# One tile for both parts of A, half as many copies, and output stores issued five slots later

## The chip, the cores and the metric

The kernel runs on one core of a Trainium2 chip. The metric is the device time of one execution in microseconds, lower is better. The engines are called by the profile's names: PE (TensorE, the matmuls), DVE (VectorE), ACT (ScalarE), POOL (GpSimd) and SP (SyncE, which here issues nearly all DMAs). SPq is SP's queue of DMA issues.

## The reference

Two attention steps over 32 inducing points, then a feed-forward layer with a leaky ReLU (slope 0.01). `x` is 4 x 12480 x 128, `w_in` 128 x 2048, `w_out` 2048 x 128, the output 49920 x 128.

```python
def mab(q, kv):                       # I is the 32 inducing rows, for each of 4 batches
    s = scale * (q @ kv.transpose(0, 2, 1))
    s = s - s.max(-1, keepdims=True)
    a = np.exp(s)
    a /= a.sum(-1, keepdims=True) + 1e-09
    return a @ kv
h = mab(I, x)                         # 32 x 128 for each batch
y = mab(x, h).reshape(49920, 128)     # attention of each token over 32 rows
t = y @ w_in
out = np.maximum(0.01 * t, t) @ w_out
```

## The kernel before

**What is computed where.** The second attention's weights (32 numbers a token, the matrix A) are not multiplied by h first. The kernel forms h @ w_in for each batch, so that the hidden layer of 512 tokens is a product with the 32 rows of A, and splits each factor into a high and a low part, for three products where one would be too coarse. The leaky ReLU is a ReLU part (`ghi`, `glo`) and a linear part (0.01 t, from A and a product of all weights). On PE a matmul uses a quarter of the array (32 rows), and four streams, r = 0 to 3, take turns on the four quarters; so A must stand in all four groups of 32 partitions.

**Tiles, slots and turns.** A batch has six groups of 2048 tokens (four tiles of 512) and a remainder of 192. The remainders of two batches make a *pair tile*; there are 98 tiles in all, two of them pairs (tiles 28 and 77). The first two tiles ("quick") and the last go another way. For each of the 95 others, the hidden layer is walked in 16 *slots* (f = 0 to 15), about a microsecond each. `row_group(r)` is the order of one stream: "first" makes the hidden part, "second" multiplies it by `w_out`, and first runs four to eight slots ahead of second.

**The background work.** After each slot `next_slot` gives every background lane a step: `stacking`, `stores`, `seconds` (the second attention of later groups), `scores` and `values` (the first attention of the next batch, with its loads `xc` and `xr`). A lane is a list of Python generators; one step runs the first generator to its next `yield`. A lane's step can be put off by `debt` (a heavy step before) and by the quiet slots f = 0 to 3, of which only f = 3 steps `stores`. All this fixes the order of each engine's instructions when the program is built; each engine then runs its own list in order and waits on semaphores.

**The stack.** `stack` takes the four tiles of a group (or one pair): ACT copies the rounded weights into `ahi` (L735), POOL subtracts into `alo` (L740), and for each tile SP copies 32 partitions of each part to the four partition groups of an `A4` tile (L755), eight DMAs a tile. `ahi` and `alo` have one buffer each, so the next stack's L735 and L740 can run only when the copies of the last tile before have landed. There are three `A4` buffers. A pair tile has six parts of 64 tokens, so 48 small DMAs.

**The end of a tile.** `gather` adds the four streams' sums: ACT copies r = 0 and r = 2 into `part` (two buffers), DVE adds r = 1 and r = 3, POOL adds the two. Before a new copy into `part`, it steps the lane of stores until no total is still waiting for its transposition (`while unsaved: step(stores)`). `store` then lets three slots pass, transposes the total on DVE into `osb` (two buffers, L920) and issues four DMAs to the output on SP (L935); 24 small ones for a pair.

Of the kernel before, what the change touches and what calls it, by code (L numbers as in the profile page):

```python
# [9 lines left out]
F32 = mybir.dt.float32  # L10
F32R = mybir.dt.float32r
# [8 lines left out]
def induced_attention_then_leaky_ffn(  # L20
# [20 lines left out]
    nc = tc.nc  # L41
    B, N, C = x.shape
    M = inducing.shape[0]
    DFF = w_in.shape[1]
    P = 128
    NF = DFF // P
    TOK = 512
# [41 lines left out]
    QUICK = 2  # L89
# [3 lines left out]
    GB = 7  # L93
    AHEAD = 4
    LAG = 1
    debt = [0]

    const = ctx.enter_context(tc.tile_pool(name="const", bufs=1))
    sb = ctx.enter_context(tc.tile_pool(name="sb", bufs=2))
# [20 lines left out]
    def done(t, later=6):  # L120
        i = next(i for i in range(8) if banks[i] is t)
        held.discard(i)
        if quads[0]:
            free.append((turn[0] + later, i))
            free.sort()

    def aux_ps(name):
        return bank("aux")
# [593 lines left out]
    def stack(tiles_, eng=None):  # L722

        while not all(s[:2] in aT for t in tiles_ for s in t[1]):
            yield
        ahi = sb.tile([P, TOK], F32R, tag="ahi", name="ahi", bufs=1)
        alo = sb.tile([P, TOK], F32R, tag="alo", name="alo", bufs=1)
        at = {}
        for _, parts in tiles_:
            for b, g, *_ in parts:  # L730
                if (b, g) not in at:
                    at[b, g] = sum(32 * GROUPS[q][2] for _, q in at)
        for (b, g), o in at.items():
            _, J, K = GROUPS[g]
            nc.scalar.copy(ahi[: 32 * J, o : o + 32 * K], aT[b, g][: 32 * J, :])  # L735
        yield
        for (b, g), o in at.items():
            _, J, K = GROUPS[g]
            sl = (slice(0, 32 * J), slice(o, o + 32 * K))
            (eng or nc.gpsimd).tensor_tensor(  # L740
                out=alo[sl], in0=aT.pop((b, g))[: 32 * J, :], in1=ahi[sl].bitcast(F32),
                op=ALU.subtract,
            )
        yield
        for t, parts in tiles_:
            while len(A4) >= A4_BUFS:
                yield
            a4 = sb.tile([P, 2, TOK], F32R, tag="A4", name="A4", bufs=A4_BUFS)
            to = 0
            for b, g, js in parts:  # L750
                w, o = 32 * GROUPS[g][2], at[b, g]
                for j in js:
                    for which in range(2):
                        for r in range(4):
                            nc.sync.dma_start(  # L755
                                a4[32 * r : 32 * r + 32, which, to : to + w].bitcast(F32),
                                (ahi, alo)[which][32 * j : 32 * j + 32, o : o + w].bitcast(F32),
                            )
                    to += w
                    yield  # L760
            A4[t] = a4

    def quick(t):

        b, g, (j,) = tiles[t][0]
        hT = hw[b][0]
        sp = aux_ps("q_ps")
        for c in range(4):
            nc.tensor.matmul(
                sp[:, c * M : (c + 1) * M], xT[b, g][:, j, c * P : (c + 1) * P], hT[:, :M],  # L770
                start=True, stop=True,
            )
        yield
        sv = sp[:, : 4 * M].rearrange("p (c m) -> p c m", m=M)
        mx = sb.tile([P, 4], F32, tag="mx", name="qmx")
        nc.vector.tensor_reduce(out=mx, in_=sv, op=ALU.max, axis=AX.X)
        y = sb.tile([P, 4, M], F32, tag=("ahi", "alo")[t], name="qy", bufs=1)
        nc.vector.tensor_tensor(
            out=y, in0=sv, in1=mx.unsqueeze(2).broadcast_to([P, 4, M]), op=ALU.subtract
        )  # L780
        done(sp)
        nc.scalar.activation(y, y, AF.Exp, scale=SCALE)
        yield
        sm = sb.tile([P, 4], F32, tag="sm", name="qsm")
        nc.vector.tensor_reduce(out=sm, in_=y, op=ALU.add, axis=AX.X)
        nc.vector.tensor_scalar_add(sm, sm, 1e-9)
        nc.vector.reciprocal(sm, sm)
        nc.vector.tensor_tensor(
            out=y, in0=y, in1=sm.unsqueeze(2).broadcast_to([P, 4, M]), op=ALU.mult
        )  # L790
        yield
        pa = bank("out")
        for c in range(4):
            for r in range(4):
                nc.tensor.matmul(
                    pa[32 * r : 32 * r + 32, c * P : (c + 1) * P], y[:, c, :], ident,
                    start=True, stop=True, tile_position=(0, 32 * r),
                )
        yield
        A4[t] = a4 = sb.tile([P, 2, TOK], F32R, tag="A4", name="A4", bufs=A4_BUFS)  # L800
        nc.scalar.copy(a4[:, 0, :], pa)
        yield
        nc.vector.tensor_tensor(
            out=a4[:, 1, :], in0=pa, in1=a4[:, 0, :].bitcast(F32), op=ALU.subtract
        )
        done(pa)
        yield
# [11 lines left out]
    def spans(t):  # L819

        got, at = [], 0
        for b, g, js in tiles[t]:
            n = len(js) * 32 * GROUPS[g][2]
            got.append((b, at, n))
            at += n
        return got, at
# [88 lines left out]
    def store(t, total, summed):  # L915
        _, n = spans(t)
        if summed:
            yield from idle(3)
        osb = sb.tile([P, TOK], F32, tag="osb", name="osb", bufs=2)
        nc.vector.transpose(osb[:, :n], total[:, :n])  # L920
        if summed:
            unsaved.remove(t)
        else:
            done(total)
        yield HEAVY
        o = 0
        for b, g, js in tiles[t]:
            base, J, K = GROUPS[g]
            n = 32 * K
            for j in js:  # L930
                row = b * N + base + j * 32 * K
                dst = out[row : row + n, :].rearrange("(r k) c -> r k c", k=K)
                for cb in range(NB):

                    (nc.scalar if t == NT - 1 and cb % 2 else nc.sync).dma_start(  # L935
                        dst[:, :, 32 * cb : 32 * cb + 32],
                        osb[32 * cb : 32 * cb + 32, o : o + n].rearrange("p (k c) -> p k c", c=32),
                    )
                o += n
            yield  # L940
# [10 lines left out]
    def idle(n):  # L951
        for _ in range(n):
            yield
# [35 lines left out]
    with tc.manual_schedule():  # L989
# [102 lines left out]
        def row_group(r):  # L1092

            todo = []
            for i, (t, f) in enumerate(work):
                if f % 4 == r:
                    todo.append((i - AHEAD - FURTHER * (r == FAR), 0, "first", t, f))
                todo.append((i + LAG * r, 1, "second", t, f))
                if r != t % 4 and f == (3 if t > QUICK + 3 else NF - 1):
                    todo.append((i + LAG * r + 0.5, 2, "linear", t, (r - t) % 4 - 1))  # L1100
            todo.sort()
# [70 lines left out]
        t = NT - 1  # L1172
# [45 lines left out]
```

## Time and profile before

| what | value |
|---|---|
| median of three runs | 1670.46 us (1669.81 to 1673.67) |
| the profiled execution's own time | 1674.81 us |
| its span, first to last instruction | 1672.7 us |
| mean granted clock of PE | 0.966 |
| PE busy | 1562.8 us, 93% of the span |
| DVE, ACT, POOL busy | 1163.7, 1066.9, 941.7 us |
| share of the chain that ended last on PE, on the SP queue | 79%, 11% |

A row of groups has the line, engine and operation, the tiles (out<-in), the form and the count, then busy time and mean ns of one, then the idle time before them and what ended it. A row of waits has the total, the number and the longest wait in us. A row of a timeline has start and length in us; x4 means four instructions merged into it, and square brackets hold idle time ahead. A row of windows has, after the window and its length, the busy time and count of PE, PEld (weight loads), DVE, ACT and POOL, then the granted clock, the DMA engines' share and GB/s.

### The profile page before, as it was taken

Reading aid. Unit: us, or ns where it says so; the run is one execution under the profiler, and the core shown is the slowest. Engines: PE = TensorE matmul, PEld = TensorE weight load, DVE = VectorE, ACT = ScalarE, POOL = GpSimd, SP = SyncE. Lnnn points to the kernel's source line nnn. Section 1 sums busy time; section 2 is a strip of 40 time slices with the busy share of each in tenths; the row PEclk is TensorE's granted clock in tenths of the full one; section 3 lists DMA queues with packets and bytes.
Section 4 is the critical chain, followed back from the end, with each engine's and each line's share of the span. In section 5 each row is a group of like instructions: output and inputs, shape, how many; then the busy total and the mean of one; then the engine's idle time right before and its main releaser. Section 6 shows DMA issues by size and latency. Waiting matters only on the chain.

```text
span 1672.7 us, 60122 instructions
## 1 busy us (share of the span) xinstructions
PE 1562.8 (93%) x25047; PEld 1353.4 (81%) x25047; DVE 1163.7 (70%) x2046; ACT 1066.9 (64%) x1957; POOL 941.7 (56%) x963
## 2 busy tenths in 40 slices
PE   8999999999966899999996999999999598999997
PEld 5678888888855778888886888878889497999996
DVE  6677788767744667776774788767777376766664
ACT  6456677676733566666674676667677365777773
POOL 2146666566633555565664675555666465666663
PEclk9899999999977999999998999999999799999998
DMA  7155544422333244443224444553222122222221
GB/s 256 18 116 94 109 100 99 103 54 54 60 79 67 49 96 101 98 90 77 53 51 99 74 81 101 105 120 77 53 51 54 33 45 55 59 59 59 58 47 20
DMA packets 419520, 128.52 MB, mean 77 GB/s; under 512 B 379920, under 2 KB 382384, under 8 KB 419248
## 3 DMA queue, kind: packets, MB, share of 16 engines
q1 hardware_dynamic: 418144, 124.53, 35.8%
q8 instruction: 197, 3.23, 0.8%
q14 instruction: 75, 0.61, 0.1%
q10 hardware_dynamic: 1104, 0.15, 0.1%
HBM read 48.94 MB, written 25.56 MB: 45 GB/s over the span
## 4 chain that ended last, share of the span: by engine, by line
PE 79%; SPq 11%; DMA 3%; DVE 3%; issue 2%; POOL 1%; ACT 1%; ACTq 0%; DVEq 0%; POOLq 0%
PE bank L874 72%; SPq L755 4%; SPq L320 3%; SPq L935 3%; PE bank L334 2%; PE bank L900 2%; PE bank L458 1%; DMA xr<-in_x_dram 1%; DVE glo L852 1%; DMA A<-ahi 1%; POOL glo L845 1%; DMA raw<-in_moe_w_in_dram 1%; ACT ghi L849 0%; DMA A<-alo 0%; PE bank L365 0%
## 5 line engine op out<-in xcount | busy, mean ns | idle before, releaser
L874 PE MATMUL bank<-ghi,w_hi 32*128 32x512 f32 x6080 | 1295.8, 394 | 0.6 <-DVE part L1157 0.4
L874 PE MATMUL bank<-glo,w_hi 32*128 32x512 f32 x6080 | 1295.1, 393 | 0.2 <-DVE glo L852 0.2
L874 PE MATMUL bank<-ghi,w_lo 32*128 32x512 f32 x6080 | 1294.5, 394 | 0.0
L874 PE MATMUL bank<-A,hwhi 32*128 32x512 f32 (+1 forms) x3394 | 1136.0, 394 | 68.1 <-ACT g L842 62.4
L852 DVE SCALAR_TENSOR_TENSOR glo<-bank,ghi 128x512 fp32r<-128x512 f32 x1184 | 796.1, 681 | 350.7 <-ACT ghi L849 344.4
L849 ACT ACTIVATE ghi<-bank 128x512 fp32r<-128x512 f32 x1184 | 701.6, 598 | 296.1 <-PE bank L874 269.8
L874 PEld LDWEIGHTS bank<-ghi,w_hi 32*128 32x128 f32 x6080 | 847.3, 185 | 46.5 <-issue 17.6
L874 PEld LDWEIGHTS bank<-glo,w_hi 32*128 32x128 f32 x6080 | 850.0, 185 | 27.3 <-DVE glo L852 0.6
L874 PEld LDWEIGHTS bank<-ghi,w_lo 32*128 32x128 f32 x6080 | 849.4, 185 | 25.0
L874 PEld LDWEIGHTS bank<-A,hwhi 32*128 32x128 f32 x3394 | 586.2, 185 | 115.1 <-ACT g L842 66.6
L874 PE MATMUL bank<-A,hwlo 32*128 32x512 f32 (+1 forms) x1697 | 642.5, 391 | 0.0
L845 POOL TENSOR_TENSOR glo<-g,ghi 128x512 fp32r<-128x512 f32 (+1 forms) x384 | 495.7, 1291 | 30.7
L844 POOL CAST ghi<-g 128x512 fp32r<-128x512 f32 (+1 forms) x384 | 234.1, 610 | 407.1 <-ACT g L842 339.2
L874 PEld LDWEIGHTS bank<-A,hwlo 32*128 32x128 f32 x1697 | 307.4, 185 | 7.6
L842 ACT ACTIVATE g<-bank 128x512 f32<-128x512 f32 (+1 forms) x384 | 229.4, 597 | 126.3 <-PE bank L874 120.0
L1161 POOL TENSOR_TENSOR part<-part 128x512 f32<-128x512 f32 (+1 forms) x95 | 122.6, 1290 | 109.1 <-DVE part L1157 109.1
L1157 DVE TENSOR_TENSOR part<-bank,part 128x512 f32<-128x512 f32 (+1 forms) x190 | 130.2, 685 | 57.4 <-PE bank L874 46.2
L1154 ACT COPY part<-bank 128x512 f32<-128x512 f32 (+1 forms) x190 | 110.4, 581 | 35.7 <-PE bank L874 35.0
L740 POOL TENSOR_TENSOR alo<-aT,ahi 128x512 fp32r<-128x512 f32 x24 | 31.0, 1291 | 83.0 <-DMA A<-alo 45.8
L735 ACT CAST ahi<-aT 128x512 fp32r<-128x512 f32 x24 | 14.8, 615 | 88.7 <-DMA A<-ahi 78.2
L920 DVE STREAM_TRANSPOSE osb<-part 128x512 f32<-128x512 f32 (+1 forms) x95 | 66.3, 698 | 0.0
L439 DVE STREAM_TRANSPOSE xT<-xc 128x512 f32<-128x512 f32 x72 | 50.3, 698 | 0.0
(120 smaller groups left out, 644.6 us busy)
## 6 DMA issues: line engine op xcount, KB each, us to landing
xr<-in_x_dram SPq DMA_DIRECT2D x96, 256.0 KB, 4.8
out_dram<-osb SPq DMA_DIRECT2D x382, 64.0 KB, 2.2
A<-ahi SPq DMA_DIRECT2D x376, 64.0 KB, 2.0
A<-alo SPq DMA_DIRECT2D x376, 64.0 KB, 2.0
xc<-in_x_dram SPq DMA_DIRECT2D x288, 64.0 KB, 2.7
raw<-in_moe_w_in_dram SPq DMA_DIRECT2D x4, 512.0 KB, 6.7
raw<-in_moe_w_out_dram SPq DMA_DIRECT2D x4, 512.0 KB, 7.4
A<-ahi SPq DMA_DIRECT2D x48, 8.0 KB, 1.8
```

Of the source, the lines that this page charges most:

```text
L439: nc.vector.transpose(t[:, j, :], blk.rearrange("p n c -> p (n c)"))
L755: nc.sync.dma_start(a4[32 * r : 32 * r + 32, which, to : to + w].bitcast(F32), (ahi, alo)[which][32 * j : 32 * j + 32, o : o + w].bitcast( ...
L842: nc.scalar.activation(g[:, :n], ph[:, :n], AF.Relu)
L844: nc.gpsimd.tensor_copy(ghi[:, :n], g[:, :n])
L845: nc.gpsimd.tensor_tensor(out=glo[:, :n], in0=g[:, :n], in1=ghi[:, :n].bitcast(F32), op=ALU.subtract)
L849: nc.scalar.activation(ghi[:, :n], ph[:, :n], AF.Relu)
L852: nc.vector.scalar_tensor_tensor(out=glo[:, :n], in0=ph[:, :n], scalar=0.0, in1=ghi[:, :n].bitcast(F32), op0=ALU.max, op1=ALU.subtract,)
L874: nc.tensor.matmul(dst, w[32 * r : 32 * r + 32], x[32 * r : 32 * r + 32], start=start, stop=stop, tile_position=(32 * r, 0),)
L920: nc.vector.transpose(osb[:, :n], total[:, :n])
L1154: nc.scalar.copy(part[:, :n], po[:, :n])
L1157: nc.vector.tensor_tensor(out=part[:, :n], in0=po[:, :n], in1=part[:, :n], op=ALU.add)
L1161: nc.gpsimd.tensor_tensor(out=total[:, :n], in0=total[:, :n], in1=part[:, :n], op=ALU.add)
```

## The change

`ahi` and `alo` become the two halves of one tile `both`, and one DMA copies both parts of 32 partitions into an `A4` tile: four DMAs of 128 KB a tile where there were eight of 64 KB, and 24 for a pair where there were 48. Quick's two scratch tiles, which used the places of `ahi` and `alo`, share a tile of the new kind. In `store`, five more steps of the lane pass between the transposition and the DMAs.

```diff
+    STORE = 5
...
-        ahi = sb.tile([P, TOK], F32R, tag="ahi", name="ahi", bufs=1)
-        alo = sb.tile([P, TOK], F32R, tag="alo", name="alo", bufs=1)
+        both = sb.tile([P, 2, TOK], F32R, tag="both", name="both", bufs=1)
+        ahi, alo = both[:, 0, :], both[:, 1, :]
...
-                    for which in range(2):
-                        for r in range(4):
-                            nc.sync.dma_start(
-                                a4[32 * r : 32 * r + 32, which, to : to + w].bitcast(F32),
-                                (ahi, alo)[which][32 * j : 32 * j + 32, o : o + w].bitcast(F32),
-                            )
+                    for r in range(4):
+                        nc.sync.dma_start(
+                            a4[32 * r : 32 * r + 32, :, to : to + w].bitcast(F32),
+                            both[32 * j : 32 * j + 32, :, o : o + w].bitcast(F32),
+                        )
...
-        y = sb.tile([P, 4, M], F32, tag=("ahi", "alo")[t], name="qy", bufs=1)
+        if not qys:
+            qys.append(sb.tile([P, QUICK, 4, M], F32, tag="both", name="qy", bufs=1))
+        y = qys[0][:, t]
...
         yield HEAVY
+        if summed:
+            yield from idle(STORE)
         o = 0
```

In the changed kernel the copies stay at L755, the stores stand at L941, the transposition at L924, and gather's copy and add at L1160 and L1163. How the change moves instructions is shown at three places.

SP's queue where the loads of the third batch come in (`xc`, `xr`), ahead of the first pair's copies; before:

```order
L935 DMA out_dram<-osb 512x1x32 x4
L320 DMA xc<-in_x_dram 32x2x32 x12
L320 DMA xc<-in_x_dram 32x16x32 x16
L310 DMA xr<-in_x_dram 96x256
L310 DMA xr<-in_x_dram 128x512 x4
L755 DMA A_9373<-ahi 32x512 x4
L755 DMA A_9373<-alo 32x512 x4
L935 DMA out_dram<-osb 512x1x32 x4
L320 DMA xc<-in_x_dram 32x16x32 x8
L755 DMA A_9731<-ahi 32x512 x4
L755 DMA A_9731<-alo 32x512 x4
```

The same place after:

```order
L941 DMA out_dram<-osb 512x1x32 x4
L321 DMA xc<-in_x_dram 32x2x32 x12
L321 DMA xc<-in_x_dram 32x16x32 x16
L311 DMA xr<-in_x_dram 96x256
L311 DMA xr<-in_x_dram 128x512 x4
L755 DMA A_9282<-both 32x1024 x4
L941 DMA out_dram<-osb 512x1x32 x4
L321 DMA xc<-in_x_dram 32x16x32 x8
L755 DMA A_9638<-both 32x1024 x4
L941 DMA out_dram<-osb 512x1x32 x4
L755 DMA A_10002<-both 32x2x64 x24
```

The rows keep their places, with four copies for eight, but each store is that of the tile before: the first row stores tile 22 before and tile 21 after.

SP's queue at the output of the first pair tile, the 24 small stores; before:

```order
L755 DMA A_11274<-ahi 32x512 x4
L755 DMA A_11274<-alo 32x512 x4
L935 DMA out_dram<-osb 64x1x32 x24
L320 DMA xc<-in_x_dram 32x16x32 x8
L755 DMA A_11663<-ahi 32x512 x4
L755 DMA A_11663<-alo 32x512 x4
```

The same place after:

```order
L755 DMA A_11155<-both 32x1024 x4
L321 DMA xc<-in_x_dram 32x16x32 x8
L941 DMA out_dram<-osb 512x1x32 x4
L321 DMA xc<-in_x_dram 32x16x32 x8
L755 DMA A_11520<-both 32x1024 x4
L311 DMA xr<-in_x_dram 128x512 x4
L941 DMA out_dram<-osb 64x1x32 x24
L755 DMA A_11920<-both 32x1024 x4
```

The 24 stores stood ahead of the copies of tile 32 (A_11663), the last of its stack, and stand behind them now (A_11520).

DVE's list at the gathering of a tile (the adds into `part`, two of each tile) and the transposition of a total into `osb`; before:

```order
L1157 TENSOR_TENSOR part<-bank_67,part 128x512
L852 SCALAR_TENSOR_TENSOR glo<-bank_66,ghi 128x512
L852 SCALAR_TENSOR_TENSOR glo<-bank_69,ghi 128x512
L1157 TENSOR_TENSOR part<-bank_68,part 128x512
L852 SCALAR_TENSOR_TENSOR glo<-bank_71,ghi 128x512
L852 SCALAR_TENSOR_TENSOR glo<-bank_69,ghi 128x512
L852 SCALAR_TENSOR_TENSOR glo<-bank_68,ghi 128x512
L920 STREAM_TRANSPOSE osb<-part 128x512
```

The same place after:

```order
L856 SCALAR_TENSOR_TENSOR glo<-bank_70,ghi 128x512
L856 SCALAR_TENSOR_TENSOR glo<-bank_71,ghi 128x512
L924 STREAM_TRANSPOSE osb<-part 128x512
L1163 TENSOR_TENSOR part<-bank_66,part 128x512
L856 SCALAR_TENSOR_TENSOR glo<-bank_67,ghi 128x512
L856 SCALAR_TENSOR_TENSOR glo<-bank_71,ghi 128x512
L1163 TENSOR_TENSOR part<-bank_64,part 128x512
```

The transposition stood three rows behind a tile's own second add and stands now just ahead of the next tile's first add; in ACT's list one of the next tile's two copies into `part`, the second, now waits for DVE.

More of the change, by code (lines that the diff above doesn't have):

```diff
@@ L761, in stack @@
             A4[t] = a4
+    qys = []
     def quick(t):
```

## The prediction

> **What bounds the kernel now.** First the page's busy shares and the idle time before the groups of TensorE, then the list of waits, then windows cut around the idle places, and last the timeline of the SP queue ahead of them.
>
> ```profile
> PE 1562.8 (93%) x25047; PEld 1353.4 (81%) x25047; DVE 1163.7 (70%) x2046; ACT 1066.9 (64%) x1957; POOL 941.7 (56%) x963
> ...
> ACT ahi L735 <- DMA A<-ahi: 93.9, 8, 18.9
> ...
> PE bank L874 <- ACT g L842: 62.4, 6, 16.7
> ...
> PE bank L334 <- DVE glo L852: 17.8, 1, 17.8
> ```
>
> TensorE is busy for 93% of the span, and what it waits for longest (62.4 us in only six waits, 17.8 in one) are relu results of ACT and DVE. ACT is not slow: it stands at L735, the copy of a new stack's high part, until the DMAs that still read the old stack have landed (93.9 us in eight waits). Nine windows take in every idle place of TensorE after the start that is over 1 us, except the program's end; the last row is a stretch without any.
>
> ```profile
> 461.00:484.00 23.00, 8.70 (x114) 6.91 (x110) 4.68 (x9) 4.65 (x10) 4.25 (x6) 0.64 0.55 117
> 500.00:526.00 26.00, 9.32 (x105) 7.39 (x101) 5.69 (x11) 6.18 (x12) 5.97 (x6) 0.61 0.20 39
> 576.00:594.00 18.00, 7.79 (x96) 6.08 (x88) 4.71 (x9) 4.51 (x9) 4.20 (x5) 0.72 0.46 81
> 654.00:662.00 8.00, 6.49 (x78) 4.72 (x76) 3.15 (x5) 4.26 (x8) 4.95 (x5) 0.79 0.47 95
> 717.00:727.00 10.00, 8.07 (x138) 5.60 (x135) 4.21 (x11) 4.46 (x9) 4.57 (x5) 1.00 0.62 142
> 902.00:925.00 23.00, 9.11 (x123) 8.07 (x120) 5.60 (x10) 5.03 (x11) 5.00 (x5) 0.70 0.57 119
> 1106.00:1116.00 10.00, 6.49 (x92) 3.73 (x88) 3.15 (x9) 2.68 (x5) 3.10 (x3) 0.83 0.52 100
> 1313.00:1338.00 25.00, 7.17 (x88) 4.30 (x84) 2.66 (x5) 3.71 (x8) 5.02 (x5) 0.66 0.19 36
> 1386.00:1400.00 14.00, 7.92 (x108) 6.71 (x104) 3.77 (x7) 3.99 (x8) 4.65 (x6) 0.76 0.35 69
> sum 157.00, PE 71.06 PEld 53.52 DVE 37.63 ACT 39.47 POOL 41.71; mean PE 7.90 PEld 5.95 DVE 4.18 ACT 4.39 POOL 4.63
> ...
> 1475.00:1635.00 160.00, 160.00 (x2750) 153.74 (x2745) 112.75 (x171) 115.82 (x207) 103.45 (x105) 1.00 0.27 55
> ```
>
> The nine windows are 157.0 us long and TensorE is busy for 71.1 of them, so 85.9 us are idle. They hold 942 matmuls (the sum of the counts); at the 2750 in 160 us of the last row, 17.2 a us, these need 54.8 us. So the windows lose 102.2 us: 85.9 idle and 16.3 at the lower granted clock (0.61 to 0.83 in eight of them, 1.00 in the last row). If all of it went, the span of 1672.7 would be 1570.5. The profiled execution took 1674.81 us, 4.35 over the median of 1670.46; I take what is saved off the median, which makes the floor 1568.3.
>
> What the DMAs wait for is the SP queue. Its timeline ahead of the first loss, and ACT's rows at L735 at the six large ones (start, length, then the idle time ahead):
>
> ```profile
> 433.90 3.25 SPq L935 DMA_DIRECT2D out_dram<-osb  x4
> 437.20 20.41 SPq L320 DMA_DIRECT2D xc<-in_x_dram  x28
> 457.65 3.36 SPq L310 DMA_DIRECT2D xr<-in_x_dram  x5
> 461.11 2.44 SPq L755 DMA_DIRECT2D A<-ahi  x4
> 463.60 2.50 SPq L755 DMA_DIRECT2D A<-alo  x4
> 466.19 2.63 SPq L935 DMA_DIRECT2D out_dram<-osb  x4
> 468.87 5.32 SPq L320 DMA_DIRECT2D xc<-in_x_dram  x8
> 474.29 2.47 SPq L755 DMA_DIRECT2D A<-ahi  x4
> ...
> 478.38 0.39 ACT L735 CAST ahi<-aTr 96x64 fp32r<-96x64 f32 x2 [15.74 <-DMA A<-ahi]
> ...
> 517.44 0.62 ACT L735 CAST ahi<-aT 128x512 fp32r<-128x512 f32 x1 [18.48 <-DMA A<-ahi]
> ...
> 587.87 0.62 ACT L735 CAST ahi<-aT 128x512 fp32r<-128x512 f32 x1 [12.58 <-DMA A<-ahi]
> ...
> 919.15 0.62 ACT L735 CAST ahi<-aT 128x512 fp32r<-128x512 f32 x1 [16.25 <-DMA A<-ahi]
> ...
> 1332.28 0.62 ACT L735 CAST ahi<-aT 128x512 fp32r<-128x512 f32 x1 [18.90 <-DMA A<-ahi]
> ...
> 1394.20 0.62 ACT L735 CAST ahi<-aT 128x512 fp32r<-128x512 f32 x1 [8.21 <-DMA A<-ahi]
> ```
>
> SP issues back to back from 433.9 to 476.8, each DMA 0.6 to 0.65 us after the last (2.44 for four, 20.41 for 28). ACT was ready at 478.38 - 15.74 = 462.6, but the last tile of the old stack had its copies issued only from 474.29. TensorE loses about 1.8 us less than ACT waits (15.74 gave an idle 23.00 - 8.70 = 14.3; 18.90 gave 25.00 - 7.17 = 17.8): so much work lies ahead of it.
>
> **The merged copy.** It removes 424 issues on SP, half of all copies: 376 of the whole tiles (row below) and 48 of the two pair tiles. Whether a DMA of 128 KB is issued as fast as one of 64 KB no row shows; the bounds are these:
>
> ```profile
> A<-ahi SPq DMA_DIRECT2D x376, 64.0 KB, 2.0
> ...
> xr<-in_x_dram SPq DMA_DIRECT2D x96, 256.0 KB, 4.8
> ...
> 489.20:510.80 21.60, 13.24 (x227) 10.67 (x223) 9.31 (x16) 7.71 (x15) 7.99 (x8) 0.86 0.07 14
> ...
> 1583.50:1588.50 5.00, 5.00 (x93) 5.00 (x89) 2.90 (x5) 3.86 (x7) 2.36 (x3) 1.00 0.49 109
> ```
>
> Four xr loads of 256 KB and a smaller one took 3.36 us above, 0.67 each with a pause among them: bytes do not set the issue time. I take 0.63 us, so 2.5 us a tile instead of 5.0; the other end is 1.25 us, with nothing saved. Landing lies between 2.0 us (64 KB) and 4.8 (256 KB); I take 2.4, near the first, since the eight copies of a tile, one each 0.63 us, fill only 0.49 of the DMA engines (last row), so twice the bytes in that time just fit. Bytes stay the same in all.
>
> The row of 489.2 to 510.8 is a pair tile's 48 copies of 8 KB: issues at full cadence, and the DMA engines 0.07 busy. The Trainium skill, "DMA: Bandwidth & Descriptors", section "Issuing engines are not separate DMA queues", says that the sequencer's time to start a DMA is usually small beside the DMA itself. By that, halving the issues would bring nothing and only the moved stores count; the 0.07 speaks against it here. The second rival below has the time that this would give.
>
> **The later store.** `store` now takes 11 steps of its lane where it took 6, and a tile has 16 slots, some of them barred. So the next tile's store starts late, `gather` forces its transposition, and the DMAs come a whole tile later than before, against every other queue entry. The SP queue no longer stands waiting for a fresh transposition: ahead of the 28 loads it must now wait for the one that stands at the gathering before (its second ACT copy, the first one at 426.40), not for that at 433.2.
>
> ```profile
> 426.40 0.59 ACT L1154 COPY part<-bank 128x512 f32<-128x512 f32 x1 [0.35 <-PE bank L874]
> 428.71 0.58 ACT L1154 COPY part<-bank 128x512 f32<-128x512 f32 x1
> ...
> 866.49 0.58 ACT L1154 COPY part<-bank 128x512 f32<-128x512 f32 x1
> ...
> L920 DVE STREAM_TRANSPOSE osb<-part 128x512 f32<-128x512 f32 (+1 forms) x95 | 66.3, 698 | 0.0
> ```
>
> The cost is that the second copy into `part` waits for this transposition (it writes the buffer that is read). DVE needs 0.70 us for it and starts it ahead of the first copy's time, so it ends near 427.4, 1.3 us before the second copy at 428.71. Per tile I put the loss at 0.05 us, between 0 and the 0.7 of a transposition that starts when the copy is due; about 75 of the 95 tiles have it so close in the order of the instructions, hence 4 us, with 0 and 52 as ends. `osb` has two buffers and its DMAs now end about 20 slots before the next use instead of 30, so no wait. Quick's shared tile costs nothing: both are read and gone long before the first stack. The final tile's store is not delayed.
>
> **Each loss again, with these prices.** At 462.6: store after the transposition at 427.5, until 430.1; the 33 loads take 461.11 - 437.20 = 23.9, until 454.0; one tile's copies 2.5, a store 2.6, eight loads 5.3, the last tile's copies 2.5, until 466.9, landed near 468.9. ACT waits 6.3, TensorE 4.5. At 902.9 (919.15 - 16.25) the same from 867.5: 2.6, 22.4 (loads and their pauses), 2.5, 2.6, 5.3, 2.5 end at 905.4, landed at 907.4; ACT waits 4.5, TensorE 2.7.
>
> The pair tile: 48 copies become 24. The next rows are the first and the last four high-part copies of the second pair and the 24 stores of its output.
>
> ```profile
> 1298.75 2.46 SPq L755 DMA_DIRECT2D A<-ahi  x4
> ...
> 1328.31 2.49 SPq L755 DMA_DIRECT2D A<-ahi  x4
> ...
> 1373.37 16.54 SPq L935 DMA_DIRECT2D out_dram<-osb  x24
> ```
>
> They can start when the low part is made, near 1296.5; 24 x 0.63 = 15.1 and one store of 2.6 end at 1314.2, landed 1.5 later (now the last are issued by 1330.8 and release ACT at 1332.28): ACT, ready at 1332.28 - 18.90 = 1313.4, waits 2.3, TensorE 0.5 instead of 17.8. The first pair starts once ACT is free at 468.9 and ACT and POOL have split the new stack, 2 us that I estimate from ACT's 0.39; 15.1 on and 1.5 to land make 487.5. ACT gets there at 517.44 - 18.48 = 499.0 now, and 9.8 earlier (14.3 idle become 4.5), at 489.2, then: 0 instead of 16.7. The 24 stores of a pair's output now stand behind the last tile's copies: the loss at 1394 (6.1) goes, that at 588 (10.2) shrinks: 16.5 us of stores leave the queue ahead of ACT's 12.6 us wait, eight loads of 5.3 come in, the copies take 2.5 less, which would end it; as these loads wait for buffers that DVE frees, I leave 0.9. The three small losses (1.5, 1.9, 3.5 idle) lose half of a tile's 5.0 us: 0, 0 and 0.6. Left idle: 4.5 + 2.7 + 0.5 + 0.9 + 0.6 = 9.2. For the clock I leave 1.7 us at three of them, 5.1, as the window of 654 to 662 has it: (1 - 0.79) x 8.
>
> The Trainium skill, "TensorE: Matmul & The Clock Gate", Part 1, has the clock halve only after an idle window of about 3.4 us. By it only the loss of 4.5 would cost clock and the sum would be some 3 us less; the window of 654 to 662, with 1.5 us idle and 0.79, does not agree.
>
> Sum: 102.2 - 9.2 - 5.1 - 4 = 83.9 saved; 1670.5 - 83.9 = 1587.
>
> **Rivals.** First, the transposition at the gathering reaches TensorE at 0.2 to 0.5 us a tile, through DVE running late: 75 tiles make 15 to 37 us, 1601 to 1623. For it: DVE and ACT are near 70% in the clean stretch (112.75 and 115.82 of 160). Against: 1.3 us of room. Second, a merged issue takes twice as long, so only the moved stores help: the boundary waits are each 5 us longer, the pair tiles keep 30 us of issues and idle about 9 and 14, in all some 43 us idle, 9 of clock and 9 for the rest: 41 saved, 1629. Against it are the xr rows. Third, everything goes: 1568 to 1573, if TensorE's lead covers the waits of 4 to 6 us. The one on the other side: DVE reaches the forced transposition so late that TensorE pays each time. That outweighs 88 us from 1.2 us a tile on 75 tiles; at 1.5 it would be 1670.5 - 88 + 112 = 1695. It needs DVE 2.5 us behind at each gathering, which no row here shows. Last, that the store moves without effect and the copies were not on the path: the chain through L735 speaks against it.
>
> **Chances.** Forecast 0.66 (1574 to 1600), first rival 0.12, second 0.10, third 0.07, slower 0.03, within 0.3% (1665.5 to 1675.5, what a measurement tells from none) 0.02. From 1569 to 1628 lie the forecast, the first rival and half of the second and third, over 8 in 10. Faster 0.95.
>
> **What would show it.** Right: SP's merged copies 2.5 us for four; L735's waits under 7 us, two of them left; the window list above with under 12 us idle; the second L1160 copy never waiting over 1 us for DVE. Wrong: four merged copies taking 5 us; waits at L735 that stay over 10; TensorE idle spread over all tiles, released by ACT or DVE.

## The result, and the profile after

| kernel | median, us | range | ratio to before, 95% interval |
|---|---|---|---|
| before | 1672.07 | 1669.81 to 1673.79 | |
| changed | 1620.67 | 1618.41 to 1625.50 | 0.9697 [0.9671, 0.9724] |

The change makes the kernel 3.0% faster, 51 us, where 84 were forecast. The profiled execution took 1625.50 us, with a span of 1623.7 us against 1672.7: 49.0 us less. From the page of the changed kernel, the busy line and the shares of the chain that ended last:

```profile
PE 1571.7 (97%) x25047; PEld 1339.5 (82%) x25047; DVE 1157.0 (71%) x2046; ACT 1068.4 (66%) x1957; POOL 943.3 (58%) x963
...
PE 82%; DVE 6%; POOL 4%; issue 3%; ACT 2%; SPq 1%; DMA 1%; ACTq 0%; DVEq 0%; POOLq 0%
```

The SP queue's share of the chain fell from 11% to 1%; DVE's rose from 3% to 6%. PE is busy for 9 us longer than before, with the same number of matmuls. The waits (total in us, number, longest) show what left and what came:

```profile
PEld bank L878 <- DVE glo L856: 49.7, 75, 3.9
...
ACT both L736 <- DMA A<-both: 23.7, 5, 8.2
...
PE bank L878 <- DVE glo L856: 17.2, 23, 3.4
PE bank L878 <- ACT g L846: 12.9, 5, 5.4
```

ACT's wait for the old stack's copies is down from 93.9 us to 23.7, and PE's wait for ACT's `g` from 62.4 to 12.9. The wait for DVE's `glo` went the other way. Before, these two rows read:

```profile
PEld bank L874 <- DVE glo L852: 23.1, 40, 2.3
...
PE bank L874 <- DVE glo L852: 5.0, 7, 1.9
```

Of the nine windows of the prediction three are left:

```profile
480.00:492.00 12.00, 6.75 (x74) 3.83 (x66) 2.50 (x5) 2.94 (x7) 3.64 (x6) 0.78 0.56 101
884.00:900.00 16.00, 10.61 (x102) 6.67 (x101) 4.22 (x8) 4.37 (x8) 5.59 (x6) 0.68 0.55 105
1289.00:1299.00 10.00, 6.58 (x84) 5.03 (x80) 4.31 (x8) 4.02 (x8) 5.88 (x6) 0.83 0.27 58
```

ACT's timeline has its copies of a new stack in them (start, length, and in brackets the wait):

```profile
487.40 0.39 ACT L736 CAST both<-aTr 96x64 fp32r<-96x64 f32 x2 [8.17 <-DMA A<-both]
...
890.53 0.62 ACT L736 CAST both<-aT 128x512 fp32r<-128x512 f32 x1 [8.18 <-DMA A<-both]
...
1293.27 0.62 ACT L736 CAST both<-aT 128x512 fp32r<-128x512 f32 x1 [4.54 <-DMA A<-both]
```

Counted as in the prediction (17.2 matmuls a us), these 38.0 us hold work for 15.1: lost are 14.1 idle and 8.8 at the lower clock, 22.9 together.

The rest is found tile by tile. The matmuls bank<-ghi,w_hi are 64 to a tile, so that their order gives the time at which each slot began in either kernel. The difference in length between two slots, changed less before, in us:

```
start to slot 48                          +3.2
slots 48 to 400    (22 tiles)            +13.0
slots 400 to 512   (losses at 462 to 588)  -37.4
slots 512 to 800   (losses at 654, 717)    -0.4
slots 800 to 832   (loss at 902)           -5.8
slots 832 to 992                          +2.6
slots 992 to 1008  (loss at 1106)          -4.3
slots 1008 to 1200                        +4.5
slots 1200 to 1280 (losses at 1313, 1386) -24.7
slots 1280 to 1540 (no background work)   +0.3
```

The boundaries gained 72 us, and stretches that had lost nothing before became longer. The clearest is the first, slots 48 to 400 (windows of before, then of the changed kernel):

```profile
114.30:455.10 340.80, 340.09 (x5689) 296.45 (x5685) 262.96 (x460) 236.33 (x432) 214.20 (x219) 1.00 0.41 84
```

```profile
117.50:471.30 353.80, 348.05 (x5695) 289.49 (x5694) 263.44 (x465) 237.52 (x433) 216.01 (x221) 1.00 0.42 83
```

It has the same number of matmuls within 6 and DVE's busy time within 0.5 us, and is 13.0 us longer. Only 5.0 of these are PE's idle time (5.75 against 0.71). Of the other 8 some 1.7 are clock: the 1.00 of the long row is rounded, and from 229 to 236 us the clock was 0.76 (a row at the end of this text shows it). The rest is "busy". Four streams share PE, and while one waits for its `glo` the others go on: PE counts as busy with less of it at work. What DVE did there at a gathering, in the changed kernel (idle time ahead would stand in brackets):

```profile
198.52 0.70 DVE L440 STREAM_TRANSPOSE xT<-xc 128x512 f32<-128x512 f32 x1
199.14 0.67 DVE L924 STREAM_TRANSPOSE osb<-part 128x512 f32<-128x512 f32 x1
199.74 0.65 DVE L1163 TENSOR_TENSOR part<-bank,part 128x512 f32<-128x512 f32 x1
200.31 1.27 DVE L856 SCALAR_TENSOR_TENSOR glo<-bank,ghi 128x512 fp32r<-128x512 f32 x2
201.51 0.67 DVE L1163 TENSOR_TENSOR part<-bank,part 128x512 f32<-128x512 f32 x1
202.11 0.67 DVE L856 SCALAR_TENSOR_TENSOR glo<-bank,ghi 128x512 fp32r<-128x512 f32 x1
202.70 0.69 DVE L440 STREAM_TRANSPOSE xT<-xc 128x512 f32<-128x512 f32 x1
203.38 0.69 DVE L856 SCALAR_TENSOR_TENSOR glo<-bank,ghi 128x512 fp32r<-128x512 f32 x1
```

At a gathering near there before the change, the transposition (L920) stood 5 us behind the second add:

```profile
194.78 0.69 DVE L1157 TENSOR_TENSOR part<-bank,part 128x512 f32<-128x512 f32 x1 [0.45 <-PE bank L874]
195.39 1.34 DVE L852 SCALAR_TENSOR_TENSOR glo<-bank,ghi 128x512 fp32r<-128x512 f32 x2
196.65 0.68 DVE L1157 TENSOR_TENSOR part<-bank,part 128x512 f32<-128x512 f32 x1
...
201.57 0.69 DVE L920 STREAM_TRANSPOSE osb<-part 128x512 f32<-128x512 f32 x1
```

In the changed kernel the forced transposition (L924) and the two adds (L1163) stand within 3.1 us, with background work (L440) on either side, and DVE has no pause in them: five operations of 0.7 us that are not `glo` among four that are. That is theory 1: this clump makes `glo` late. Its rivals were that the background work, which moved to earlier slots too, does it (theory 2; of DVE's 574 background instructions 335 stand in another tile than before), and that the merged copies do (theory 3).

### The profile page after: what moved, and what is told of

Same layout as the page of the kernel before. It is cut to its first block, busy times and chain, and to the rows that moved or that the text cites. A ratio compares the mean times of both kernels' runs of the same rounds, so it can differ in the third digit from the quotient of the medians.

```text
span 1623.7 us, 59550 instructions
## 1 busy us (share of the span) xinstructions
PE 1571.7 (97%) x25047; PEld 1339.5 (82%) x25047; DVE 1157.0 (71%) x2046; ACT 1068.4 (66%) x1957; POOL 943.3 (58%) x963
## 4 chain that ended last, share of the span: by engine, by line
PE 82%; DVE 6%; POOL 4%; issue 3%; ACT 2%; SPq 1%; DMA 1%; ACTq 0%; DVEq 0%; POOLq 0%
PE bank L878 75%; PE bank L335 3%; DVE glo L856 2%; POOL glo L849 2%; PE bank L904 2%; PE bank L459 1%; POOL ghi L848 1%; DVE part L1163 1%; SPq L755 1%; ACT ghi L853 1%; DMA A<-both 1%; POOL y L710 1%; PE bank L366 0%; POOL y L696 0%; DVE e L347 0%
## 5 line engine op out<-in xcount | busy, mean ns | idle before, releaser
L878 PE MATMUL bank<-ghi,w_hi 32*128 32x512 f32 (+1 forms) x6080 | 1294.8, 393 | 2.2 <-DVE glo L856 1.7
L878 PE MATMUL bank<-ghi,w_lo 32*128 32x512 f32 (+1 forms) x6080 | 1292.0, 393 | 0.0
L878 PEld LDWEIGHTS bank<-ghi,w_hi 32*128 32x128 f32 x6080 | 842.1, 184 | 51.1 <-issue 14.3
L1163 DVE TENSOR_TENSOR part<-bank,part 128x512 f32<-128x512 f32 (+1 forms) x190 | 129.2, 680 | 33.5 <-PE bank L878 21.0
L1160 ACT COPY part<-bank 128x512 f32<-128x512 f32 (+1 forms) x190 | 110.5, 581 | 26.1 <-PE bank L878 24.8
L924 DVE STREAM_TRANSPOSE osb<-part 128x512 f32<-128x512 f32 (+1 forms) x95 | 65.9, 694 | 0.0
L440 DVE STREAM_TRANSPOSE xT<-xc 128x512 f32<-128x512 f32 x72 | 50.2, 697 | 0.0
L741 POOL TENSOR_TENSOR both<-aT,both 128x512 fp32r<-128x512 f32 x24 | 31.1, 1295 | 29.2 <-ACT both L736 25.1
L690 DVE STREAM_TRANSPOSE y<-bank 128x512 f32<-128x512 f32 (+1 forms) x28 | 18.1, 647 | 21.3 <-PE bank L335 21.3
```

Of the source, the lines that this page charges most:

```text
L440: nc.vector.transpose(t[:, j, :], blk.rearrange("p n c -> p (n c)"))
L878: nc.tensor.matmul(dst, w[32 * r : 32 * r + 32], x[32 * r : 32 * r + 32], start=start, stop=stop, tile_position=(32 * r, 0),)
L1160: nc.scalar.copy(part[:, :n], po[:, :n])
L1163: nc.vector.tensor_tensor(out=part[:, :n], in0=po[:, :n], in1=part[:, :n], op=ALU.add)
```

## The experiments

**The parts of the change, each alone.** The first kernel has the changed kernel's copies and no delay of the stores; the second has the delay and the eight copies.

```diff
 first kernel: the changed one with
-    STORE = 5
+    STORE = 0
 second kernel: the one before with
+    STORE = 5
...
         yield HEAVY
+        if summed:
+            yield from idle(STORE)
```

> The merged copies alone: the stores follow their transposition at once, as in the kernel before, and every instruction but the A copies stands in the slot where it stood before. Theory 1 (in the changed kernel the transposition is forced onto the gathering of the next tile, DVE's work stands there in a clump and its glo comes late by fractions of a microsecond on many tiles): no clump here, so the clump's 15 to 25 us are not paid, but SP still waits at fresh transpositions and five of the nine windows keep a part of their stall (11.6, 10, 10.7, 6 and 0.5 us, and 11 us of half clock). Worked out: 52 us saved, 1620 us, between 1612 and 1632. The rows would show ACT's wait for the DMAs of the old stack at 35 to 50 us in all (93.9 before) and PE's wait for glo as before (about 5 us on PE, 23 us on PEld). Theory 2 (what is lost is lost to background work that stands earlier in the changed kernel, since the debt of the transposition falls into quiet slots): the same here, since the background stands as before. Theory 3 (the merged copies themselves cost PE, by their bytes or their landing): slower than 1640 us, and PE's small waits as in the changed kernel.

Measured: 1644.36 us (1642.60 to 1646.38), ratio 0.9821 [0.9803, 0.9840]. The waits of ACT and PE:

```profile
ACT both L736 <- DMA A<-both: 70.8, 11, 14.1
...
PEld bank L878 <- DVE glo L856: 23.5, 41, 2.3
...
PE bank L878 <- DVE glo L856: 5.0, 7, 1.8
```

The waits for `glo` are those of before to within 0.4 us, and the stretch of slots 48 to 400 is 0.2 us longer than before, so the merged copies cost PE nothing (theory 3 falls). The size was missed by 24 us: ACT's waits stayed at 70.8 us, where 35 to 50 were expected.

> The later stores alone: eight copies a tile from two tiles, and five slots between the transposition and its stores. Theory 1: the clump is here in full, as in the changed kernel (PE's and PEld's waits for glo about 17 and 50 us, 5 and 23 before), while the copies take 5 us a tile as before; some 41 us of the nine windows go, 15 to 25 us come back: 1650 us, between 1640 and 1662. Theory 2: the same, since the background moves as in the changed kernel. Theory 3 (the merged copies cost PE): no clump, PE's waits for glo as before, 1630 us or less.

Measured: 1659.49 us (1655.13 to 1661.34), ratio 0.9908 [0.9882, 0.9934], inside the range of theories 1 and 2.

```profile
PEld bank L875 <- DVE glo L853: 58.9, 69, 15.6
PE bank L875 <- DVE glo L853: 28.6, 22, 15.1
```

The waits for `glo` rise without a merged copy (one of 15 us among them belongs to a boundary). So the later store pays and costs: 15 us gained alone; the merged copies bring 30 us alone, and some 35 behind later stores (from the ratios 0.9908 and 0.9697; the kernel before was measured anew with each group of runs, and its medians differ by 2.7 us).

**The transposition or the background work.** In the third kernel the stores' DMAs are issued from a lane of their own, so nothing forces the transposition. The fourth is the changed kernel with the debt charged later.

```diff
 third kernel
+        while len(outs) > 1:
+            step(outs)
         osb = sb.tile([P, TOK], F32, tag="osb", name="osb", bufs=2)
...
-            yield from idle(STORE)
+            outs.append(issue(t, osb, STORE + 2 * (len(tiles[t]) > 1)))
+        else:
+            yield from issue(t, osb, 0)
 (issue(t, osb, later) idles `later` steps, then issues the DMAs; STORE = 6;
  the lane outs is stepped once a slot, behind that of the stacks)
 fourth kernel
+        yield
+        if summed:
+            yield from idle(3)
         yield HEAVY
         if summed:
-            yield from idle(STORE)
+            yield from idle(1)
```

> Merged copies and later stores, but the transposition where it stood before: three steps after the sums, not forced by the gathering of the next tile, since the stores have a lane of their own and are issued 8 to 25 slots behind their transposition (13 in the mean, in the changed kernel 10). The background work (loads of xc and xr, scores, values) stands in the slots where it stood before. Theory 1: the relief at the boundaries of the changed kernel is kept and the clump on DVE is gone, so PE's and PEld's waits for glo fall back to about 5 and 23 us; 15 to 25 us faster than the changed kernel, 1600 us, between 1594 and 1608. Theory 2 (it is the background that moved): as fast, since the background stands as before too; the fourth kernel tells the two apart. Theory 3 (neither; the residue belongs to the merged copies or the late stores themselves): within 5 us of the changed kernel, 1616 to 1626 us.

Measured: 1609.17 us (1607.58 to 1609.95), ratio 0.9610 [0.9593, 0.9626]; by the ratios some 14.6 us faster than the changed kernel (11.5 by the medians). The clean stretch of slots 48 to 400 is as long as before the change, 340.70 us:

```profile
116.00:456.70 340.70, 339.99 (x5689) 297.09 (x5685) 263.15 (x460) 236.72 (x432) 214.35 (x219) 1.00 0.45 88
```

Each tile in it is as long as before to 0.1 us. The gain is smaller than the spread price that went, since a new loss came: the first pair's late stores hold an `osb` that DVE needs. PE's and PEld's waits for `glo` are 15.9 and 35.2 us, where about 5 and 23 were expected; 8.3 and 8.7 of them are this one stall.

```profile
575.70 0.71 DVE L926 STREAM_TRANSPOSE osb<-part 128x512 f32<-128x512 f32 x1 [9.22 <-DMA out_dram<-osb]
```

> The changed kernel with one edit: the debt of the transposition is charged three steps of the lane later. The transposition is still forced onto the gathering (77 of 95 within one slot of it, 63 in the changed kernel), the stores stand as late as there, but the background work (xc, xr, scores, values) stands again where it stood in the kernel before (it was 9 to 15 slots earlier in the changed kernel). Theory 1 (the forced transposition): as slow as the changed kernel, 1614 to 1628 us, PE's waits for glo at 17 and 50 us. Theory 2 (the background that moved): 15 to 25 us faster, about 1600 us, between 1594 and 1608, and PE's waits for glo back at 5 and 23 us.

Measured: 1623.08 us (1621.58 to 1625.53), ratio 0.9695 [0.9677, 0.9714], as slow as the changed kernel. In its profile 539 of DVE's 574 background instructions stand in the tile where they stood before, and slots 48 to 400 still take 11.0 us longer. Theory 2 falls as the whole cause: with the background back in its place the price stays while the transposition is forced, and in the third kernel it goes. How much of it hangs on the background's place is not settled: the waits for `glo` fell part of the way (10.1 us on PE and 34.9 on PEld, where 17 and 50 were expected), and ACT has two long waits at a new stack's copy in this stretch (3.06 us at 162.71 and 2.50 at 230.01, where the longest before was 0.70). That the route is DVE's list is read from the rows.

**What the boundaries still cost.** In undisturbed stretches of before, ACT's copy of a new stack starts 5 to 7 us behind the issue of the old stack's last copies, and SP's first copy of the new stack is issued 10 to 15 us behind it. So the copy should be able to stand later with little or nothing needing it:

```diff
 def stack(tiles_, eng=None):
         while not all(s[:2] in aT for t in tiles_ for s in t[1]):
             yield
+        if tiles_[0][0] > 4 + QUICK:
+            yield from idle(4 if len(tiles[tiles_[0][0] - 1]) > 1 else 8)
```

It was put into the kernel before, the merged copies alone (the expectations call this one the eighth kernel), the third kernel and the changed one.

> The kernel before (eight copies a tile, stores behind their transposition) with one edit: the copy of a new stack on ACT, and POOL's subtraction with it, are put eight steps of their lane later (four after a pair), about 8 us. Every other instruction stands in the slot where it stood. The new stack's first copy by SP comes 14 slots after the old stack's last, so nothing needs the copy sooner. Theory A (the whole loss at the boundaries is ACT standing in its list at a copy that nobody needs yet, while SP works off its queue): SP's issues are as slow and as late as before, yet most of the loss goes: of ACT's eight waits, 93.9 us in all, each loses some 8 us, 30 to 40 us stay; saves 65 to 80 us, 1600 us, between 1588 and 1615. Theory B (SP's queue itself bounds these windows, whoever waits for it: if ACT doesn't wait at the old copies, PE waits soon after for the new ones): the loss moves to PE's waits for DMAs into A, and at most 25 us are saved, over 1645 us.

Measured: 1639.85 us (1637.69 to 1642.18), ratio 0.9787 [0.9772, 0.9801]: 35 us faster, between both theories and nearer theory B's bound.

```profile
482.54 0.39 ACT L737 CAST ahi<-aTr 96x64 fp32r<-96x64 f32 x2 [8.09 <-DMA A<-ahi]
...
519.54 0.62 ACT L737 CAST ahi<-aT 128x512 fp32r<-128x512 f32 x1 [21.79 <-DMA A<-ahi]
```

The wait ahead of the pair fell from 15.7 to 8.1 us as theory A has it, but that behind it rose from 18.5 to 21.8: there four steps are too few while SP works off the pair's 48 copies. Theory B's shift is there but small: PE waits for copies into A, for which it hadn't waited before, for 1.7 us in all.

> Merged copies alone (stores behind their transposition at once, the transposition where it stood before) and ACT's copy of a new stack eight steps of the lane later. Theory A: ACT's waits for the old stack's copies, 70.8 us in 11 with the merged copies alone and at most 14.1, fall to under 10 us; no clump on DVE and no late store; 1577 us, between 1570 and 1588, 55 to 75 us faster than the merged copies alone. Theory B: within 20 us of the merged copies alone, over 1624 us.

Measured: 1609.66 us (1607.37 to 1611.55), ratio 0.9606 [0.9592, 0.9620]; 35 us gained, not 55 to 75; ACT still waits 28.3 us for copies into A, where under 10 were expected.

> The kernel with merged copies, stores in a lane of their own (13 slots late) and the transposition where it stood before, and ACT's copy of a new stack eight steps later. Theory A: ACT's waits for the old stack's copies are gone (21.0 us without the edit). What stays is DVE's wait for a free osb behind the first pair's late stores (9.2 us at 575.7 us), which PE feels with 8.3 us and a stretch of half clock: 1586 us, between 1576 and 1594, slower than the eighth kernel by about 10 us, that is, with the copy later the late stores no longer pay. Theory B: no faster than 1604 us.

Measured: 1600.05 us (1596.62 to 1600.79), ratio 0.9545 [0.9531, 0.9559]; slower than expected by 14 us; ACT's waits for copies into A, expected gone, are 10.3 us.

> The changed kernel with ACT's copy of a new stack eight steps later and nothing else. Theory A with theory 1 of the first runs (the transposition forced onto the gathering costs 11 to 20 us by itself, most of it between 115 and 470 us): the stalls at 488 and 892 us go (5.25 and 5.39 us and their half clock), the clump stays: 1596 us, between 1588 and 1606, slower than the eighth kernel by 12 to 22 us. If the clump cost only where the boundaries were tight: within 6 us of the eighth kernel.

Measured: 1608.93 us (1605.46 to 1611.03), ratio 0.9606 [0.9590, 0.9622]. It ties with the eighth, which the last sentence of the expectation had for the case that the clump costs only where boundaries are tight. It is a coincidence of two prices: slots 48 to 400 were 7.7 us longer than before here and 0.1 us shorter there, while the eighth lost more at the boundaries.

The same stretch is 13.0 us longer in the changed kernel. The 5.3 us that went stand in two tiles, 3.7 at slot 144 and 1.6 at slot 208. There ACT waited at a new stack's copy in the changed kernel, and has no such wait here:

```profile
225.61 0.62 ACT L736 CAST both<-aT 128x512 fp32r<-128x512 f32 x1 [1.69 <-DMA out_dram<-osb]
293.01 0.62 ACT L736 CAST both<-aT 128x512 fp32r<-128x512 f32 x1 [2.33 <-DMA A<-both]
```

The first is put down to a store; which DMA held it the row doesn't settle. PE was idle for 1.02 and 1.14 us behind them (at 230.4 and 294.2), and the stretch of 0.76 clock lies behind the first. So 5.3 of the 13.0 us are not the transposition's alone: they need ACT's early copy too.

All four missed for one reason, three mainly and the eighth by half (17.6 of 32.7 us, by the kernel that mends it below), and the length of the tiles at the boundaries shows it (us; the tiles at 432 and 1216 come behind the pairs):

```
slot   before  merged alone  changed   merged alone,  merged alone,  changed,   apart,
                                       copy later     also at pairs  at pairs   at pairs
 400    33.4      31.9         25.1        18.1           18.5          17.0      16.3
 416    32.1      19.2         14.9        20.6           19.8          14.9      14.3
 432    19.3      19.1         18.4        23.9           17.0          18.4      17.1
 480    30.2      29.6         19.5        17.4           17.4          18.9      17.4
 496    16.1      16.1         14.9        18.0           18.4          14.9      25.0
 800    30.5      27.6         26.6        18.5           16.1          17.1      14.2
 816    17.1      16.1         15.1        22.8           24.0          15.2      16.1
1200    34.6      21.5         18.2        15.6           15.6          14.5      15.6
1216    14.5      15.7         16.8        22.1           14.0          15.4      14.0
```

The loss ahead of a pair came back behind it (432 and 1216: 23.9 and 22.1 us in the fourth column of times, 40.1 and 33.6 in the kernel before with the later copy, 24.4 and 18.9 in the third, 22.0 and 22.9 in the changed one). That place has less slack in the program, not in the data: the copy there can stand ten steps later too. The last three columns are kernels with `idle(10 if ... else 8)`. In the last of them the first pair's 24 stores are also issued in one go, at slot 492.

> Merged copies alone and ACT's copy of a new stack later, now behind the pairs too (ten steps there instead of four; eight elsewhere as before). In the run with four steps the loss that had stood ahead of the pair came back behind it: the tile that begins at slot 432 took 23.9 us and that at slot 1216 22.1, where about 15.5 and 14.5 are free of stalls, since ACT meets the stack behind the pair while SP still works at the pair's 24 copies. Theory A (ACT stands at a copy that nobody needs yet): these two tiles fall to 15 to 17 us, 1594 us, between 1588 and 1602. Theory B (the loss moves on to the next place at which SP's lateness is felt, PE's own wait for the new stack's copies): the sum stays within 4 us of 1609.7.

Measured: 1592.05 us (1589.89 to 1594.27), ratio 0.9508 [0.9486, 0.9529]. The two tiles fell to 17.0 and 14.0 us; of the stalls that are left the largest is at the loads of a batch (slot 816, 24.0 us), where the kernels with later stores have none.

> The changed kernel with the same edit (eight steps, ten behind a pair). Tiles at slots 432 and 1216 took 22.0 and 22.9 us with four steps. Theory A: they fall to 15 to 17 us; no stall over 2 us is left between 100 and 1570 us; the forced transposition's spread price stays (8 to 13 us between slots 48 and 400, some 6 us behind). 1595 us, between 1590 and 1603. Theory B: within 4 us of 1608.9.

Measured: 1596.79 us (1594.02 to 1597.20), ratio 0.9537 [0.9514, 0.9560]. ACT waits for no copy into A any more, and PE's waits are these:

```profile
PEld bank L880 <- DVE glo L858: 45.3, 71, 2.3
...
PE bank L880 <- DVE glo L858: 14.8, 22, 1.8
...
PE bank L880 <- ACT g L848: 0.2, 1, 0.2
```

So here the price of the forced transposition stands without waits for copies. PE and PEld wait for `glo` in 22 and 71 small pieces, and the stretches outside the boundaries are 20 us longer than before: 7.7 in slots 48 to 400, 2.8 in 512 to 540, 2.3 in 640 to 800, 2.6 in 832 to 992, 4.1 in 1008 to 1200 and 0.4 from 1280. Of the 7.7, some 6.6 stand in the first half of the 22 tiles, where DVE had 22.5 instructions a tile before the change, against 19.2 in the second half.

> Merged copies, stores in their own lane, transposition where it stood before, ACT's copy later (eight steps, ten behind a pair), and the first pair's 24 stores issued in one go at slot 492, where they came in two halves at 493 and 500. Theory A: no spread price, tiles 432 and 1216 at 15 to 17 us (24.4 and 18.9 with four steps behind a pair), and DVE's wait for a free osb behind the pair's stores down from 10.5 to about 5 us (tile 496 from 28 to about 22 us): 1581 us, between 1574 and 1590, the fastest of all, 10 to 20 us ahead of the other two. Theory B: within 4 us of 1600.

Measured: 1581.54 us (1580.33 to 1583.18), ratio 0.9446 [0.9425, 0.9466], the fastest, 94 us less than before. Beside the start and the end its one stall of over 1 us is the `osb` again, with 7.5 us where about 5 were expected:

```profile
566.40 0.71 DVE L928 STREAM_TRANSPOSE osb<-part 128x512 f32<-128x512 f32 x1 [7.53 <-DMA out_dram<-osb]
```

It beats the kernel with the forced transposition by 15.3 us (1596.79 - 1581.54), although it has this stall and that one hasn't; the two differ in their lane of stores too. Theory A held in all three; of theory B's shift a little is left where the stores come at once (PE waits 3.4 us for copies into A in the first of the three).

## Why the prediction was right, and by how much it missed

**The number: inside the range, by way of a rival.** 1620.67 us lies in 1569 to 1628, but outside the forecast's own 1574 to 1600, to which I gave 0.66; it is inside because the range took in the first rival (1601 to 1623). The direction and the main mechanism held, the size of the gain did not: 51 of 84 us. Of the four signs that I named for being right, two came (merged copies at 2.5 us for four, no wait of the second copy into `part`), and two did not: five waits at L736 are left, up to 8.2 us, and 14.1 us idle in the windows, where I had two under 7 and under 12.

**The bound and the mechanism: right.** ACT standing at the new stack's copy behind SP's queue was what the nine windows lost. Two kernels show it: shorter queues took the loss away (the changed one), and so did a later copy with the queue left as it was (the kernel before, 35 us; the tiles at 400, 480, 800 and 1200 fall in every kernel with the later copy).

**The merged copy: right.** Four copies of 128 KB take 2.46 us to issue (the median of the changed kernel's 94 such groups; 2.49 for the 188 groups of 64 KB before) and land in 2.4 us. The timeline of SP's queue ahead of the first stall left:

```profile
446.18 19.28 SPq L321 DMA_DIRECT2D xc<-in_x_dram  x28
465.50 3.67 SPq L311 DMA_DIRECT2D xr<-in_x_dram  x5
469.28 2.46 SPq L755 DMA_DIRECT2D A<-both  x4
471.83 3.73 SPq L941 DMA_DIRECT2D out_dram<-osb  x4
475.67 6.50 SPq L321 DMA_DIRECT2D xc<-in_x_dram  x8
482.27 3.22 SPq L755 DMA_DIRECT2D A<-both  x4
```

and the page's row of the issues (count, size of one, median us to landing):

```profile
A<-both SPq DMA_DIRECT2D x376, 128.0 KB, 2.4
```

That excludes the second rival.

**The residues at the boundaries: somewhat too small.** The first was put at an ACT wait of 6.3 and 4.5 us idle, and is 8.17 and 5.25. The rows above show why: the 33 loads were no slower than forecast (22.95 us for 23.9), but the store (3.73 us for 2.6), the eight loads (6.50 for 5.3) and the last copies (3.22 for 2.5) were each issued more slowly. The second was 8.18 and 5.39 for 4.5 and 2.7, the pair's 4.54 and 3.42 for 2.3 and 0.5. The lead of 1.8 us that I took off ACT's waits is near the mean of the six large stalls (1.9), though the two that I quoted for it give 1.4 and 1.1; here it was 2.9, 2.8 and 1.1. Idle at the three: 14.1 us against the 9.2 left for all. At the clock they lost 8.8 against 5.1. Together 22.9 us for 14.3: 8.6 of the miss.

**The forced transposition: the step that failed.** I priced it at 0.05 us a tile by the one wait that I looked at, ACT's second copy into `part`, and there I was right: no wait of that copy for DVE is in the list. But the transposition also stands in DVE's own list, ahead of the adds and the next `glo`, and the room of 1.3 us on ACT says nothing of that. Outside the boundaries the profiled execution lost some 26 us (13.0 between slots 48 and 400; 2.8 and 3.0 in slots 512 to 540 and 640 to 800, on either side of the small losses at 654 and 717; 2.6, 4.5 and 0.3 behind), where I had 4: 22 of the miss. Some 20 of the 26 us stay in the changed kernel with the later copy at pairs too, where ACT waits for no copy: that is the transposition, 16 us more than the 4 of the sum, and 0.27 us in the mean on each of 75 tiles. That is the first rival with its mechanism and its range, to which I gave 0.12. By medians the price is 13.9 us (the fourth kernel against the third) and 15.3 us (the last pair of kernels), both with a stall of `osb` on the other side. Where there is no background work, from slot 1280, it is 0.3 us: the clean stretch whose shares of DVE and ACT I named for this rival was the one stretch that can't show it.

**New waits at stacks that had lost nothing: left out.** Most of the other 6 us (5.3) are ACT's waits of 1.69 and 2.33 us for a new stack between slots 48 and 400. The sum looked again only at the losses of before. A wait of 1.69 us would have cost TensorE nothing by the lead of 1.8 us; it came with 1.02 us idle and a stretch of 0.76 clock.

**The start.** 3.2 us of the miss lie ahead of slot 48. In the eleven other kernels this stretch was between 0.7 us shorter and 3.7 us longer than in the one trace of before, and I see no pattern in it by their edits. 8.6 + 16 + 6 + 3.2 make 34 of the 34.9 us that the span is short of the forecast (83.9 - 49.0).

**The later store: right in what it takes away.** The losses at 1394 and 588 went (tiles 1264 and 480: 24.2 to 14.4, 30.2 to 19.5 us). That `osb` suffices held too: in the changed kernel DVE waits for none. It fell in the third kernel, whose stores come later behind the transposition.

## What to carry to other kernels

When an instruction is moved, price it in the list of its own engine first, and then with those who wait for it; a moved 0.7 us on an engine at 70% cost 0.27 us a tile in the mean, and next to nothing where no other work stood around it. Before speeding up a queue that an engine waits for, look whether the engine has to ask so early: an order that lets it come eight slots later took as much from the kernel before (35 us) as the merged copies did (30 us), with two lines, and both together more than either. And a loss that goes from one place is to be looked for at the next with less slack, tile by tile.

## What the runs showed of the hardware

The busy time of PE hides waits when several streams share it: in slots 48 to 400, 340.09 us for 5689 matmuls became 345.32 us for 5696 in the changed kernel with the later copy at pairs too, at a granted clock of 1.00 all through. So idle time alone would have shown only 2.5 of 7.7 us.

```profile
113.60:462.10 348.50, 345.32 (x5696) 289.21 (x5692) 262.54 (x464) 237.04 (x433) 215.91 (x221) 1.00 0.43 84
```

Short stalls are dear in clock. In the nine windows of before, 85.9 us idle came with 16.3 us lost at the lower clock, 0.19 for each; in the three left, 14.1 came with 8.8, 0.62 for each. And a stall of 1 us can cost clock or not (in the changed kernel, one of 1.02 us at 230.4 and one of 1.40 us at 1172.9):

```profile
229.00:236.00 7.00, 5.98 (x73) 4.58 (x72) 5.31 (x10) 3.21 (x7) 3.58 (x5) 0.76 0.31 68
...
1170.00:1177.00 7.00, 5.60 (x95) 4.71 (x91) 5.25 (x11) 5.36 (x10) 3.41 (x4) 1.00 0.31 54
```

The rule of the Trainium skill that the prediction weighed ("TensorE: Matmul & The Clock Gate", Part 1: the clock halves behind an idle window of about 3.4 us) fits the three stalls of 3.42 to 5.39 us and the second of these rows, and not the first.
